# Sorting q by PSUM bank instead of by head halves, and turning the convolution weights later

## The chip, the cores and the metric

The kernel runs on one core of a Trainium2 chip. The engines named below are TensorE (PE, with its weight loads shown apart as PEld), VectorE (DVE), ScalarE (ACT), GpSimd (POOL) and SyncE (SP), which only issues transfers. Each engine takes its own instructions strictly in order. The metric is the device time of one execution in microseconds (us); lower is better.

## The reference, cut to what matters

Batch 8, 8 heads, sequence 576, head dimension 64, so that 8 x 64 = 512 columns go into the second part.

```python
kv  = einsum('bhsd,bhse->bhde', k, v)          # k^T v for each head, 64 x 64
out = einsum('bhsd,bhde->bhse', q, kv)         # "raw" in the kernel
rms = sqrt(mean(out * out, axis=-1) + 1e-6)
x   = out / rms * g_norm                       # then (B,H,S,D) -> (B,S,512)
gate = sigmoid(sum over k of conv_w[k] * x shifted by 4 - k)   # causal, 5 taps
val  = x @ w_val
result = (gate * val) @ w_out
```

The weights w_val, conv_w and w_out arrive as 64-bit floats and are made 32-bit on the chip ("narrowed") by a chain of integer and float steps on DVE and ACT. g_norm is folded into w_val and conv_w.

## The kernel before, in words

The program is one list of steps, the string `PLAN`. Each step is a small function (`sort_q 0 3` calls `sort_q(0, 3)`), and a step issues its instructions at once. So the list is the order in which each engine receives its work, written out by hand. A tile framework adds the waits between engines. All PSUM tiles come from one pool of 8 banks.

Work is done by batch; a batch has 5 chunks of the sequence, numbered 0 to 4. Chunks 0 to 3 have 128 tokens, chunk 4 has 64. Batch 0 (`WHOLE`) is treated differently from the others because it has nothing running ahead of it. Its steps at the head of the program, which the change and the prediction speak of, are these:

- `load_q_rows`, `load_half v`, `load_half k` load q, v and k of batch 0. v and k come in two halves (`v 0 0`, `v 0 1`); v is issued on ACT's queue, k on SP's. `stage_weight` loads a 64-bit weight: cw (conv_w with g_norm as its last row) on POOL's queue, w_val blocks on SP's. The loads of batch 1 follow on SP's queue.
- `turn_q_rows 0 j` (L478 to L489): PE transposes q for chunk j into one PSUM bank, `qTps` (L485). Of the bank's four blocks of 128 columns, the first two hold head half r = 0, the last two r = 1; the partitions 0 to 63 and 64 to 127 hold two different tokens of a pair (e = 0 and 1).
- `sort_q 0 j` (L494 to L506): four copies of 64 partitions from that bank into `qT` (L504), one for each r and e. Before the change ACT does the two copies with r = 0 and DVE the two with r = 1, for every chunk. For chunks 0 to 3 one copy has 256 elements a partition, for chunk 4 it has 128.
- `narrow_weight cw 0 n`: the narrowing of cw in eight parts. Parts 5, 6 and 0 are DVE's (L382, L387, L365), parts 1, 2 and 3 are ACT's (L370, L372, L374), parts 4 and 7 are DVE's (L377, L391), and the last one writes `cw`. The narrowing of w_val (`narrow_weight wval ...`) has the same lines with larger shapes.
- `start_warm`: matmuls on the identity that only keep PE occupied (L433).
- `kv_product 0 i` (L445): half i of k^T v, 72 matmuls into the two `kvps` banks. `kv_half 0 i` (L455): four copies on ACT that put this half into the block-diagonal `kvbd`.
- `raw_half 0 c i` (L533): q times k^T v for chunk c and half i of the heads. Only half 0 can run after `kv_half 0 0`; half 1 needs `kv_half 0 1`.
- `turn_cw` (L416): PE transposes `cw` into the bank `cwps`. `keep_cw` (L420 to L422): DVE takes g_norm (`gcol`) and the convolution weights (`cwT`) out of it.
- `square 0 c` (L552, ACT), `sums 0 c` (L565, DVE), `powers` (L573, POOL) and `normalise 0 c` (L582, DVE) make x; `turn_x` (L604, PE) and `keep_x` (L611, ACT) turn it for the second part.

In DVE's queue the three instructions of `keep_cw` come directly ahead of the narrowing of the first two w_val blocks (L382, L365, L387, L365, L382, L387), and these come ahead of `sums 0 3`. In ACT's queue `kv_half 0 1` is followed by parts 1 and 2 of the first w_val block (L370, L372) and then by `square 0 3`. PE goes from the raw matmuls of batch 0 straight to turning q of batch 1 (L491).

From about 30 us on the steady part follows: batch after batch of k^T v, raw, normalising, gate taps (L642, DVE), w_val products (L654, L703) and w_out products (L795, L741), interleaved by the list.

The lines that the change touches:

Of the kernel before, what the change touches and what calls it, by code (L numbers as in the profile page):

```python
# [20 lines left out]
load_half k 0 1; warm_up; stage_weight wval 1; stage_weight wval 0; start_warm 5 256; turn_q_rows 0 3;  # L21
turn_q_rows 0 2; turn_q_rows 0 0; turn_q_rows 0 1; turn_q_rows 0 4; sort_q 0 3; sort_q 0 2;
narrow_weight cw 0 5; narrow_weight cw 0 6; narrow_weight cw 0 0; sort_q 0 0; narrow_weight cw 0 1;
narrow_weight cw 0 2; narrow_weight cw 0 3; start_warm 3 256; kv_product 0 0; sort_q 0 4; kv_half 0 0;
sort_q 0 1; narrow_weight cw 0 4; narrow_weight cw 0 7; start_warm 1 256; raw_half 0 3 0; raw_half 0 4 0;
raw_half 0 2 0; turn_cw; keep_cw; kv_product 0 1; kv_half 0 1; raw_half 0 0 0; raw_half 0 1 0;
narrow_weight wval 1 5; narrow_weight wval 1 0; raw_half 0 3 1;
load_q_rows 1 1; narrow_weight wval 1 1; narrow_weight wval 1 6; narrow_weight wval 1 2; raw_half 0 4 1;
raw_half 0 2 1; load_q_rows 1 0; narrow_weight wval 0 0; narrow_weight wval 0 5; square 0 3; stage_weight wval 3;
# [180 lines left out]
def kernel(  # L210
# [11 lines left out]
    nc = tc.nc  # L222
# [45 lines left out]
    cw = const.tile([NK * K + 1, P], FP32, name="cw")  # L268
# [193 lines left out]
    def new_qT(b):  # L462
        if ("qT", b) not in st:
            st["qT", b] = work.tile([P, HP, S], FP32, tag="qT", name=f"qT{b}")
        return st["qT", b]
# [28 lines left out]
    def sort_q(b, j):  # L494

        m = min(HB, NB - j * HB)
        qT, pq = new_qT(b)[:].rearrange("p h (n t) -> p n h t", t=TB), st["pq", b, j][:].rearrange(
            "p n (h t) -> p n h t", t=TB)
        if b not in WHOLE:
            nc.scalar.copy(out=qT[:, j * HB:j * HB + m], in_=pq[:, 0:m])  # L500
            return
        for r in range(2):
            for e in range(2):
                (nc.vector.tensor_copy if r else nc.scalar.copy)(  # L504
                    out=qT[r * D:(r + 1) * D, j * HB + e:j * HB + m:2],
                    in_=pq[e * D:(e + 1) * D, r * 2:r * 2 + m // 2])  # L506

# [315 lines left out]
    def store(i, c, queue=nc.sync, blocks=range(HB)):  # L823
# [5 lines left out]
    steps = {f.__name__: f for f in (  # L829
        load_half, load_q, load_q_rows, stage_weight, narrow_weight, turn_cw, keep_cw, start_warm, warm_up,  # L830
        kv_product, kv_half, kv_copy, turn_q, turn_q_rows, sort_q, raw_half, raw_pair, raw_tail, square, sums, powers, normalise,
        turn_x, keep_x, turn_blocks, move_blocks, halo, gate_start, gate_tap, gate_end, val_product, keep_val, gated,
        val_sums, x_sums, val_fast, val_keep, out_product, keep_out, weight_sums, token_sums, fast_product, fast_keep,
# [36 lines left out]
```

## Time and profile before

| | us |
|---|---|
| median of 3 runs | 305.26 (305.22 to 305.46) |
| the profiled execution, its own time | 305.03 |
| its span, first to last instruction | 303.3 |
| PE busy | 292.9 (97% of the span) |
| PEld busy | 226.1 (75%) |
| DVE busy | 273.3 (90%) |
| ACT busy | 194.0 (64%) |
| POOL busy | 114.1 (38%) |

How to read the lines that follow: the profile gives one execution. A line of the instructions in order of time has the start in us from the span's first instruction, the length of the group, the engine, the line of the kernel (L504 is line 504), the operation, `out<-in` by the names of the tiles, the shapes (partitions x elements), how many instructions are merged, and in brackets how long the engine had been idle and what released it. PE's matmuls are pipelined, so their lengths overlap. Busy shares are means over the whole span; PE, DVE and ACT sit idle mostly in the first 30 us and at the very end.

### The profile page before, as it was taken

The page shows a single profiled execution, that of the slowest core. Times are in us where ns is not written, and L with a number is a line of the kernel's source. Part 1 is how long each engine was busy: PE and PEld are TensorE (multiplying, and loading weights), DVE is VectorE, ACT ScalarE, POOL GpSimd, SP SyncE. Part 2 cuts the span into 40 slices and gives each one's busy share as a digit, 9 for nine tenths or more (in the row PEclk, how much of TensorE's full clock was granted, in tenths as well). Part 3 has the DMA queues.
Part 4 walks back from the last instruction along what each step waited for, and adds up shares of the span by engine and source line. Part 5 has one row for each costly group of instructions (what it writes and reads, how often), then busy time and mean ns, then how long its engine had stood idle before and what let it go on. Part 6 is the DMA issues. An engine that isn't in the chain of part 4 may idle for free.

```text
span 303.3 us, 8782 instructions
## 1 busy us (share of the span) xinstructions
PE 292.9 (97%) x3333; PEld 226.1 (75%) x3333; DVE 273.3 (90%) x484; ACT 194.0 (64%) x604; POOL 114.1 (38%) x127
## 2 busy tenths in 40 slices
PE   8898999999999999999999999999999999999993
PEld 4596777787787875877778757787877588888582
DVE  1689999999999999999999999999999999999612
ACT  2679989999668654983586547682888354534220
POOL 3028073416659127265328452245536631000000
PEclk9999999999999999999999999999999999999999
DMA  7999996098469756989689477927411621112423
GB/s 274 396 400 322 278 283 166 20 281 242 130 166 352 215 143 157 285 223 267 175 238 279 126 214 189 341 57 219 108 43 35 173 73 36 35 46 61 104 69 104
DMA packets 32073, 55.51 MB, mean 183 GB/s; under 512 B 6166, under 2 KB 14358, under 8 KB 32032
## 3 DMA queue, kind: packets, MB, share of 16 engines
q1 hardware_dynamic: 29520, 49.76, 55.8%
q0 software_dynamic: 1632, 3.17, 3.9%
q10 hardware_dynamic: 880, 2.03, 1.9%
q8 instruction: 26, 0.43, 0.6%
q14 instruction: 15, 0.12, 0.2%
HBM read 39.21 MB, written 9.44 MB: 160 GB/s over the span
## 4 chain that ended last, share of the span: by engine, by line
PE 84%; DVE 6%; ACT 5%; DMA 2%; issue 2%; DVEq 0%; ACTq 0%; SPq 0%
PE a L795 18%; PE cb L795 14%; PE va L703 13%; PE val L654 11%; PE vc L703 6%; PE raw L521 5%; PE kvps L445 5%; PE out L741 5%; PE vb L703 4%; PE xTps L604 2%; DMA qs<-in_q_dram 2%; DVE gate L642 2%; DVE xs L688 1%; ACT sq L552 1%; PE raw L533 1%
## 5 line engine op out<-in xcount | busy, mean ns | idle before, releaser
L573 POOL TENSOR_TENSOR rt<-ss,mhalf 128x8 f32<-128x8 f32 (+3 forms) x38 | 68.5, 1810 | 101.2 <-DVE ss L565 101.0
L642 DVE SCALAR_TENSOR_TENSOR gate<-xT,cwT,gate 128x576 f32<-128x576 f32 x128 | 102.1, 811 | 1.0
L592 ACT ACTIVATE x<-raw,rt 128x64 f32<-128x64 f32 x252 | 55.8, 351 | 6.7 <-POOL rt L573 3.7
L625 POOL DMA_DIRECT2D xT<-y x48 | 26.4, 557 | 25.5 <-DVE ot L805 14.0
L654 PE MATMUL val<-xT,wval 128*128 128x288 f32 x128 | 33.4, 412 | 0.0
L795 PE MATMUL a<-wsum,sums 128*128 128x256 f32 x128 | 32.4, 382 | 0.0
L649 ACT ACTIVATE gate<-gate 128x576 f32<-128x576 f32 x32 | 22.0, 693 | 11.4 <-DVE gate L642 11.0
L654 PEld LDWEIGHTS val<-xT,wval 128*128 128x128 f32 x128 | 23.5, 190 | 6.9 <-DVE wval L391 0.5
L795 PEld LDWEIGHTS a<-wsum,sums 128*128 128x128 f32 x128 | 24.0, 190 | 4.1 <-issue 0.6
L556 ACT ACTIVATE sq<-raw 128x256 f32<-128x256 f32 (+1 forms) x70 | 22.2, 402 | 7.4 <-PE raw L521 7.1
L703 PE MATMUL va<-xs,vsum 128*128 128x288 f32 x96 | 26.6, 409 | 0.0
L636 ACT ACTIVATE gate<-xT,cwT 128x576 f32<-128x576 f32 x32 | 25.2, 811 | 1.4 <-DVE gv L667 1.3
L565 DVE TENSOR_REDUCE ss<-sq 128x8 f32<-128x520 f32 (+1 forms) x40 | 24.8, 630 | 1.4 <-ACT sq L552 1.0
L667 DVE TENSOR_TENSOR gv<-gv,gate 128x576 f32<-128x576 f32 x32 | 23.7, 752 | 0.9 <-ACT gate L649 0.6
L703 PEld LDWEIGHTS va<-xs,vsum 128*128 128x128 f32 x96 | 18.0, 190 | 5.2 <-ACT x L592 0.4
L632 POOL COPY xT<-xT 128x124 f32<-128x124 f32 x32 | 17.1, 575 | 9.8 <-ACT xT L611 9.8
L521 PEld LDWEIGHTS raw<-kv,qT 64*64 64x64 f32 x1008 | 16.4, 134 | 5.3 <-issue 3.0
L445 PEld LDWEIGHTS kvps<-v,k 64*64 64x64 f32 x1008 | 15.8, 135 | 4.0 <-issue 1.8
L521 PE MATMUL raw<-kv,qT 64*64 64x64 f32 x1008 | 18.7, 221 | 0.0
L445 PE MATMUL kvps<-v,k 64*64 64x64 f32 x1008 | 17.4, 220 | 0.0
L795 PE MATMUL cb<-wsum,sums 128*128 128x256 f32 x64 | 16.9, 386 | 0.1
L795 PE MATMUL cb<-wout,gv 128*128 128x256 f32 x64 | 16.8, 385 | 0.0
(114 smaller groups left out, 539.0 us busy)
## 6 DMA issues: line engine op xcount, KB each, us to landing
qs<-in_q_dram SPq DMA_DIRECT2D x96, 140.0 KB, 3.9
out_dram<-ot SPq DMA_DIRECT2D x140, 64.0 KB, 1.7
k<-in_k_dram SPq DMA_DIRECT2D x14, 576.0 KB, 6.2
v<-in_v_dram SPq DMA_DIRECT2D x12, 576.0 KB, 6.9
xT<-y SPq DMA_DIRECT2D x48, 64.0 KB, 2.5
xT<-y POOLq DMA_DIRECT2D x48, 64.0 KB, 2.9
y<-in_moe_w_val_dram SPq DMA_DIRECT2D x4, 512.0 KB, 11.2
w_wout<-in_moe_w_out_dram SPq DMA_DIRECT2D x4, 512.0 KB, 7.6
```

What stands on the lines that cost most here:

```text
L445: nc.tensor.matmul(st["kvps", b][s][r * D:(r + 1) * D, i], st["k", b, i][rows, r, cols], st["v", b, i][rows, r, cols], start=(j == 0), sto ...
L521: nc.tensor.matmul(st["raw", b, c][r][cols, to * D:(to + 1) * D], st["qT", b][rows, hp, first:first + D], kvs[b % 2][rows, hp, :], start=T ...
L565: nc.vector.reduce_sum(out=st["ss", b][:, FIRST[c]:FIRST[c] + n], in_=st["sq", b, c][:, 0:n], axis=AX.X)
L573: nc.gpsimd.tensor_tensor(out=st["rt", b][:, which], in0=st["ss", b][:, which], in1=mhalf[:, which], op=ALU.pow)
L592: nc.scalar.activation(out=x[:, to * D:(to + 1) * D], in_=raw[:, h * D:(h + 1) * D], func=AF.Copy, scale=root[:, to:to + 1])
L625: (nc.sync if i % 2 else nc.gpsimd).dma_start(out=xTs[b % 2][i * TB:(i + 1) * TB, :, first:first + P], in_=y[a * TB:(a + 1) * TB, i])
L636: nc.scalar.activation(out=gate[:], in_=xTs[b % 2][:, jt, HALO:SX], func=AF.Copy, scale=cwT[:, K - 1, jt:jt + 1])
L642: nc.vector.scalar_tensor_tensor(out=gate[:], in0=xTs[b % 2][:, jt, tap * TB:tap * TB + S], scalar=cwT[:, tap, jt:jt + 1], in1=gate[:], op ...
L654: nc.tensor.matmul(val[:], wval[:, kc, jt * P:(jt + 1) * P], xTs[b % 2][:, kc, HALO + n * SV:HALO + (n + 1) * SV], start=(kc == 0), stop=( ...
L667: nc.vector.tensor_tensor(out=both, in0=both, in1=st["gate", b, jt][:], op=ALU.mult)
L703: nc.tensor.matmul(st[bank, "val", b, mj][:], weights_[:, k], tokens()[:, k], start=(n in (0, 1, 3) and k == 0), stop=(k == NK // 2 - 1), ...
L795: nc.tensor.matmul(st[bank, i, p], tokens()[:, k], weights_[:, k], start=(n < 2 and k == 0), stop=(k == NK // 2 - 1), skip_group_check=True)
```

## The change

Two things change, both in batch 0 at the head of the program.

First, `sort_q` chooses the engine by chunk, so by PSUM bank: DVE makes all four copies of chunks 1 and 2, ACT all four of chunks 0, 3 and 4. The list moves `sort_q 0 1` ahead of `kv_half 0 0` and `sort_q 0 4` behind it.

Second, the order of raw and k^T v changes. Before: raw of chunks 3, 4, 2 (half 0), then `turn_cw`, `keep_cw`, the second k^T v, `kv_half 0 1`, raw of chunks 0 and 1. After: raw of chunks 3, 2, 0, then the second k^T v, `turn_cw`, `keep_cw`, `kv_half 0 1`, raw of chunks 1 and 4. The rest of the list is the same.

```diff
-narrow_weight cw 0 2; narrow_weight cw 0 3; start_warm 3 256; kv_product 0 0; sort_q 0 4; kv_half 0 0;
-sort_q 0 1; narrow_weight cw 0 4; narrow_weight cw 0 7; start_warm 1 256; raw_half 0 3 0; raw_half 0 4 0;
-raw_half 0 2 0; turn_cw; keep_cw; kv_product 0 1; kv_half 0 1; raw_half 0 0 0; raw_half 0 1 0;
+narrow_weight cw 0 2; narrow_weight cw 0 3; start_warm 3 256; kv_product 0 0; sort_q 0 1; kv_half 0 0;
+sort_q 0 4; narrow_weight cw 0 4; narrow_weight cw 0 7; start_warm 1 256; raw_half 0 3 0; raw_half 0 2 0;
+raw_half 0 0 0; kv_product 0 1; turn_cw; keep_cw; kv_half 0 1; raw_half 0 1 0; raw_half 0 4 0;
 narrow_weight wval 1 5; narrow_weight wval 1 0; raw_half 0 3 1;
...
         for r in range(2):
             for e in range(2):
-                (nc.vector.tensor_copy if r else nc.scalar.copy)(
+                (nc.vector.tensor_copy if j in (1, 2) else nc.scalar.copy)(
                     out=qT[r * D:(r + 1) * D, j * HB + e:j * HB + m:2],
                     in_=pq[e * D:(e + 1) * D, r * 2:r * 2 + m // 2])
```

## The prediction

> **What bounds the kernel now.** I read the page's busy shares first, then busy time by stretch, then the instructions in order of time on VectorE (DVE), ScalarE (ACT) and TensorE (PE) over the first 25 us, and last what SyncE's (SP's) queue waited for.
>
> The page, and the stretch from 32 to 80 us (busy time and count of PE, weight loads, DVE, ACT, POOL; clock; DMA share; GB/s):
> ```profile
> PE 292.9 (97%) x3333; PEld 226.1 (75%) x3333; DVE 273.3 (90%) x484; ACT 194.0 (64%) x604; POOL 114.1 (38%) x127
> ...
> 32.00:80.00 48.00, 47.98 (x664) 37.48 (x654) 47.75 (x83) 44.75 (x143) 19.47 (x14) 1.00 0.72 201
> ```
> From 32 us on PE and DVE are both full, in a written-out order that the change leaves alone there. What the head gains or loses reaches the end only as the same shift of both. The head is where both still idle. DVE in order of time (start, length, and in brackets the idle time before and what ended it):
> ```profile
> 7.64 1.75 DVE L504 COPY qT<-qTps 64x256 f32<-64x256 f32 x4 [5.92 <-ACT qT L504]
> ...
> 10.12 0.86 DVE L504 COPY qT<-qTps 64x256 f32<-64x256 f32 x2
> 11.96 0.59 DVE L504 COPY qT<-qTps 64x128 f32<-64x128 f32 x2 [0.99 <-ACT qT L504]
> 13.63 0.86 DVE L504 COPY qT<-qTps 64x256 f32<-64x256 f32 x2 [1.07 <-ACT qT L504]
> ...
> 14.82 0.28 DVE L391 SCALAR_TENSOR_TENSOR cw<-ot_cw,wexp_cw 20x128 f32<-20x128 f32 x1
> 15.44 0.16 DVE L420 TENSOR_SCALAR gcol<-cwps 128x1 f32<-128x1 f32 x1 [0.35 <-PE cwps L416]
> ...
> 19.69 0.70 DVE L565 TENSOR_REDUCE ss<-sq 128x8 f32<-128x520 f32 x1 [0.96 <-ACT sq L552]
> ```
> Each DVE copy of a bank begins 20 to 30 ns after ACT's last copy of the same bank: the two never read one bank together. The last idle time over 0.2 us is the 0.96 us before L565 (sums of chunk 3) at 19.69; after it DVE runs packed. So the start of that instruction dates everything after it. It waits for ACT's square:
> ```profile
> 6.86 2.29 ACT L504 COPY qT<-qTps 64x256 f32<-64x256 f32 x6 [3.13 <-PE qTps L485]
> 10.12 0.40 ACT L370 ACTIVATE wexp_cw<-wexp_cw,biases 20x128 uint32<-20x128 uint32 x1 [0.98 <-DVE wexp_cw L365]
> ...
> 11.40 0.53 ACT L504 COPY qT<-qTps 64x128 f32<-64x128 f32 x2
> 11.96 0.87 ACT L455 COPY kvbd<-kvps 64x64 f32<-64x64 f32 x4
> ...
> 16.66 0.87 ACT L455 COPY kvbd<-kvps 64x64 f32<-64x64 f32 x4 [3.07 <-PE kvps L445]
> 17.56 0.72 ACT L370 ACTIVATE wexp_wval<-wexp_wval,biases 128x512 uint32<-128x512 uint32 x1
> ```
> The square comes 1.50 us after the start of the L370 at 17.56, which stands behind the second kv_half (16.66), which waits for PE's second k^T v. PE:
> ```profile
> 12.43 2.16 PE L533 MATMUL raw<-kvbd,qT 128*128 128x128 f32 x12 [0.91 <-ACT kvbd L455]
> 15.20 0.21 PE L416 MATMUL cwps<-ident,cw 21*128 21x21 f32 x1 [0.61 <-PE raw L533]
> 15.34 1.28 PE L445 MATMUL kvps<-v,k 64*64 64x64 f32 x72
> 16.54 3.72 PE L533 MATMUL raw<-kvbd,qT 128*128 128x128 f32 x28
> ```
> The turning of cw (15.20) stands before the second k^T v and waits for cw, which DVE finishes at 15.10 because its sort of chunk 1 waited for ACT. So the second k^T v sits behind a sort that it doesn't need.
>
> **The change, part by part.** Sums go against the profiled execution: 305.03 us, of it 303.3 span; the median of the runs is 305.26, 0.23 above.
>
> *Copies by bank.* ACT loses 2+2 copies (r=0 halves of chunks 2 and 1) and gains 2+2 of chunks 3 and 0 and 2 of chunk 4: 8 x 0.367 + 4 x 0.26 = 3.98 against 3.46. DVE goes from 8 x 0.423 + 2 x 0.29 = 3.96 to 3.38. No copy of DVE stands behind ACT any more.
> - ACT takes chunks 3 and 0 in one run: 2.29 / 6 x 8 = 3.05, so 6.86 to 9.91.
> - DVE starts chunk 2 when PE has turned it, about 7.30 (the eighth of 18 transposes that take 2.40 from 5.95, each ending 0.27 after its start), and ends at 9.05. The three cw steps after it took 0.70 (9.39 to 10.09): 9.75. Chunk 1 follows at once and ends at 11.47.
> - ACT's three cw steps start at 9.94 (they waited for DVE until 10.12 before) and, at 1.27, end at 11.21. The first k^T v is done at 10.97, and chunk 4 is now behind kv_half: kv_half starts at 11.23 against 11.96, **0.73 earlier**. Cover: chunk 4's sort (4 x 0.27) moves to 12.10 to 13.20, where ACT sat idle (13.59 to 16.66); its reader, raw 4, now comes after the second k^T v.
> - DVE's last cw steps need ACT's (11.21) and run 11.50 to 12.10. cw is ready 3.0 us sooner.
>
> *Raw order.* Chunks 3, 2, 0 instead of 3, 4, 2. Raw starts at 12.43 - 0.73 = 11.70 (PE's warm-up ends at 11.52). Chunk 3's two waits on kvbd cost the same 0.87; the second and third chunks have 128 columns: about 0.63 each with the 0.2 us hand-over the trace shows between chunks. Second k^T v starts at 11.70 + 0.87 + 2 x 0.63 = 13.83 against 15.34, **1.51 earlier**.
>
> *cw turned behind k^T v.* In the trace the 72 matmuls take 1.20 to the next start, so cwps starts at 15.03 instead of 15.20, and L420 at 15.28 instead of 15.44: **only 0.16 earlier**. L420 to L422 stand on DVE ahead of wval's narrowing (L382, L365, L387 and so on), so DVE now idles from 12.10 to 15.28, and the narrowing is 0.16 earlier: L365 of the first weight ends at 16.57 instead of 16.73. ACT is through kv_half at 15.99, 1.54 earlier, but its L370 reads that L365: it starts at 16.60 instead of 17.56, **0.96 earlier**. Of 1.51 gained on PE, 0.55 is left at this wait.
>
> *The rest.* Square and sums follow at the old distances: L565 at 18.73. DVE's narrowings before it end at 18.57, so they don't hold it. The 28 raw matmuls run from 15.17 to 18.8; the next q loads needed there land by about 18.8 (the second issued 8.77, landed 10.0 later), and PE then waits anyway for normalise, which follows L565 through POOL's powers. PE, DVE and ACT then issue the same instructions as before, 0.96 earlier. Neither SP nor POOL issues anything differently; SP's loads of batch 2 wait for PE's turns of batch 1 and move along. Landings in the head are at full DMA share and do not move, but have room: the second half of batch 1's v lands after 11.3 us from 16.08, so about 27.4, for a product at 31.6 before, 30.7 after.
>
> Sum: 305.03 - 0.96 = 304.07; with 0.23 to the median, 304.3.
>
> *Unknown costs.* A copy with the other engine on another bank: DVE's second at 8.07 took 0.428 with ACT beside it, 0.418 to 0.428 elsewhere, so 0 to 0.05 in all; I take 0. Hand-over from raw to k^T v: between 0.11 (the pitch of matmuls) and 0.41 (the wait for data ahead of the first k^T v); I take the 0.2 seen between chunks. A head shift carried to the end: between 0 and all of it; I take all, being nearest to the row of 32 to 80 us with 0.25 us of DVE idle. A gain over 0.96 would need DVE's slack of 0.96 + 0.16 used fully: 1.12 at most. Together 303.9 to 304.7.
>
> *A landing.* The second k^T v is now asked for 1.5 us sooner. Its v half landed by 12.33, if the releaser is read rightly:
> ```profile
> SPq L312 <- DMA v<-in_v_dram: 2.0, 1, 2.0
> ```
> That is 1.5 us ahead of 13.83. The weight load issued on SP after both k halves at 2.18 landed 11.2 later, at 13.38, also ahead. What the trace proves outright is only that all was there at 15.34. The Trainium skill (DMA: Bandwidth & Descriptors, Queues, rings and completion order) says that completion is not first-in-first-out per issuing engine, so the later landing need not date the k half; but also that a DMA engine's semaphore write lands after all its earlier writes, across queues. By the first half the product could start as late as 15.33 and the time would be the 305.8 of the last rival below; by the second, which the 12.33 fits, 304.3.
>
> **The rivals.**
> - *The gain is given back.* DVE and PE run packed, but a later transfer or PSUM bank that doesn't move takes the 0.96 us: 305.2. For it: DMA is at full share up to 26 us. Against: from 26 to 60 us I find landings 3 us and more ahead of use (batch 2's last q quarter at 51.7 is turned at 60.4), and the later waits for stores are relative to DVE and ACT.
> - *More than forecast.* The 0.55 us that ACT waits shrinks, because the cw turn and L420 come sooner than I put them: up to the 1.12 of DVE's slack, 304.1; with raw's hand-overs at 0.11, too. Inside the forecast's range.
> - *Slower: DVE parks behind keep_cw.* DVE's queue now stands at L420 until the second k^T v is over. From L420's start it is 1.29 us to the end of the first L365 and, with 0.03 between, 2.13 from L370's start to L565's: 3.45 in all. So L565 is later than 19.69 as soon as L420 starts after 16.24, that is, if the second k^T v starts after 14.8. Only late data does that. At the latest start that the trace allows, 15.33, L420 is at 16.78 and the sums 0.54 late: 305.8.
> - *The change does not free DVE.* If the wait came from writing one tile qT rather than from reading one bank, DVE would still follow ACT. The changed kernel's instruction order speaks against it: its DVE copies wait for PE alone. 305.3 to 305.5.
>
> **How the numbers follow.** Forecast (with "more") 0.78; given back 0.10; parks 0.09; does not free 0.03. The forecast's own range is 303.9 to 304.7. About 0.2% (0.6 us) is what a measurement of this kernel can tell from no change. Faster by more than that: 0.76 (the forecast but for its upper edge). Within: given back, that edge and most of "not freed": 0.15. Slower: 0.09. The range reaches to the given-back case: 303.7 to 305.2.
>
> **What would show it.** In the changed profile: ACT's first group of copies is 8 long and ends near 9.9; DVE's first copy starts near 7.3 and waits for PE; kv_half near 11.2; the second k^T v near 13.8; L420 near 15.3 with some 3 us of idle before it, put down to cwps; ACT's L370 on wval near 16.6, now waiting for DVE; L565 near 18.7 with next to no idle before it; and PE's val, a and cb groups all about 1 us earlier to the end. It is wrong if the second k^T v waits for data, if L565 stays at 19.7, or if L565 is early and the same groups at 80 us or 200 us are not.

## The result, and the profile after

The changed kernel takes 304.4 us (median of 20 executions, 303.7 to 305.54), the kernel before 305.49 in the same comparison (20 executions, 305.2 to 306.56). The ratio is 0.9961, with a 95% interval of 0.9952 to 0.9971: faster by 0.4%, about 1.2 us (0.9 to 1.5 by the interval; the medians differ by 1.09). The forecast was 304.3, and 0.96 us of gain.

The profile that came with the result happens to be of the slowest of those 20 executions (305.54; its span is 303.8 us). So a second profile of the same kernel was taken (304.08 us, span 302.3), and one of the kernel before beside it (305.45, span 303.6). These two are read here, as "changed" and "before"; what the first one showed in addition comes further down.

The instructions of the changed kernel in order of time, ACT first, then DVE, then PE:

```profile
6.78 3.02 ACT L504 COPY qT<-qTps 64x256 f32<-64x256 f32 x8 [3.05 <-PE qTps L485]
9.82 0.40 ACT L370 ACTIVATE wexp_cw<-wexp_cw,biases 20x128 uint32<-20x128 uint32 x1
...
11.11 0.88 ACT L455 COPY kvbd<-kvps 64x64 f32<-64x64 f32 x4
12.01 1.08 ACT L504 COPY qT<-qTps 64x128 f32<-64x128 f32 x4
14.68 0.88 ACT L455 COPY kvbd<-kvps 64x64 f32<-64x64 f32 x4 [1.59 <-PE kvps L445]
16.15 0.72 ACT L370 ACTIVATE wexp_wval<-wexp_wval,biases 128x512 uint32<-128x512 uint32 x1 [0.60 <-DVE wexp_wval L365]
```
```profile
7.21 1.73 DVE L504 COPY qT<-qTps 64x256 f32<-64x256 f32 x4 [5.50 <-PE qTps L485]
...
9.67 1.73 DVE L504 COPY qT<-qTps 64x256 f32<-64x256 f32 x4
...
14.83 0.16 DVE L420 TENSOR_SCALAR gcol<-cwps 128x1 f32<-128x1 f32 x1 [2.81 <-PE cwps L416]
...
18.29 0.69 DVE L565 TENSOR_REDUCE ss<-sq 128x8 f32<-128x520 f32 x1 [0.17 <-ACT sq L552]
```
```profile
11.59 1.83 PE L533 MATMUL raw<-kvbd,qT 128*128 128x128 f32 x12
13.35 1.28 PE L445 MATMUL kvps<-v,k 64*64 64x64 f32 x72
14.56 0.23 PE L416 MATMUL cwps<-ident,cw 21*128 21x21 f32 x1
```

And of the kernel before, in its second profile, the points that answer to them on ACT, PE and DVE:

```profile
11.85 0.87 ACT L455 COPY kvbd<-kvps 64x64 f32<-64x64 f32 x4
...
17.46 0.72 ACT L370 ACTIVATE wexp_wval<-wexp_wval,biases 128x512 uint32<-128x512 uint32 x1
```
```profile
12.33 2.16 PE L533 MATMUL raw<-kvbd,qT 128*128 128x128 f32 x12 [0.91 <-ACT kvbd L455]
15.09 0.21 PE L416 MATMUL cwps<-ident,cw 21*128 21x21 f32 x1 [0.61 <-PE raw L533]
15.23 1.28 PE L445 MATMUL kvps<-v,k 64*64 64x64 f32 x72
```
```profile
15.34 0.16 DVE L420 TENSOR_SCALAR gcol<-cwps 128x1 f32<-128x1 f32 x1 [0.35 <-PE cwps L416]
...
19.59 0.69 DVE L565 TENSOR_REDUCE ss<-sq 128x8 f32<-128x520 f32 x1 [0.96 <-ACT sq L552]
```

What to see: DVE's copies no longer wait for ACT but for PE (the brackets), the two engines sort side by side, and kv_half starts at 11.11. The kernel before had it at 11.85. The second k^T v comes 1.88 us earlier, L420 only 0.51 earlier with 2.81 us of idle DVE ahead of it, L370 waits 0.60 us for DVE and comes 1.31 earlier, and L565 is 1.30 us earlier. In this pair of profiles that is the whole gain: the last instruction of DVE stands at

```profile
298.45 0.42 DVE L818 COPY ot<-a 128x256 f32<-128x256 f32 x1 [0.17 <-PE a L795]
```
in the kernel before, and in the changed one at
```profile
297.10 0.42 DVE L818 COPY ot<-a 128x256 f32<-128x256 f32 x1 [0.17 <-PE a L795]
```
which is 1.35 earlier. Taken every 20 us on DVE, the shift between the two profiles lies between 1.30 and 1.39 us throughout.

### The profile page after: what moved, and what is told of

It is laid out like the page before. It is cut to its first block, busy times and chain, and to the rows that moved or that the text cites. A ratio compares the mean times of both kernels' runs of the same rounds, so it can differ in the third digit from the quotient of the medians.

```text
span 303.8 us, 8778 instructions
## 1 busy us (share of the span) xinstructions
PE 293.9 (97%) x3333; PEld 226.6 (75%) x3333; DVE 273.0 (90%) x482; ACT 194.4 (64%) x606; POOL 114.5 (38%) x127
## 4 chain that ended last, share of the span: by engine, by line
PE 76%; DMA 8%; SPq 5%; ACT 4%; DVE 3%; issue 2%; DVEq 0%
PE a L795 15%; PE va L703 13%; PE cb L795 12%; PE val L654 11%; PE vc L703 6%; PE kvps L445 4%; PE raw L521 4%; DMA out_dram<-ot 4%; PE out L741 4%; PE vb L703 3%; DMA qs<-in_q_dram 3%; SPq L625 2%; PE xTps L604 2%; DMA v<-in_v_dram 2%; SPq L322 1%
## 5 line engine op out<-in xcount | busy, mean ns | idle before, releaser
L565 DVE TENSOR_REDUCE ss<-sq 128x8 f32<-128x520 f32 (+1 forms) x40 | 24.7, 627 | 0.8 <-ACT sq L556 0.7
L470 DVE STREAM_TRANSPOSE qT<-qs 128x512 f32<-128x512 f32 x24 | 16.6, 693 | 0.5 <-DMA qs<-in_q_dram 0.5
L805 DVE TENSOR_TENSOR ot<-cb,ot 128x512 f32<-128x512 f32 x16 | 10.9, 681 | 6.8 <-DMA out_dram<-ot 4.1
```

What stands on the lines that cost most here:

```text
L565: nc.vector.reduce_sum(out=st["ss", b][:, FIRST[c]:FIRST[c] + n], in_=st["sq", b, c][:, 0:n], axis=AX.X)
```

## The experiments

Absolute times in the head move by some tenths between executions: the 18 q transposes at its start take 2.18 us in one and 2.70 in another. So L565 is given here as its distance from the end of the q transposes (start plus length of PE's L485 group); it is 11.33 us for the kernel before (second profile; 11.34 in the first) and 10.03 for the changed one (9.95 in the first). The last column is the ratio of times to the kernel before on the same chip. A difference in L565 comes from one profile each, a difference in time from several executions.

| kernel | L565 after q | against before | median us (before) | ratio, 95% interval |
|---|---|---|---|---|
| before | 11.33 | | | |
| changed, second run | 10.03 | -1.30 | 304.24 (305.69) | 0.9956, 0.9942 to 0.9970 |
| banks alone | 11.02 | -0.31 | 305.05 (305.18) | 0.9994, 0.9985 to 1.0003 |
| order alone | 10.99 | -0.34 | 305.33 (305.18) | 1.0006, 0.9995 to 1.0017 |
| cw turn still later | 11.24 | -0.09 | 305.29 (305.69) | 0.9988, 0.9975 to 1.0002 |
| cw turn back ahead | 9.61 | -1.72 | 303.75 (305.18) | 0.9955, 0.9943 to 0.9967 |
| keep_cw later on DVE | 9.84 | -1.49 | 303.51 (305.18) | 0.9944, 0.9932 to 0.9956 |
| exponents early | 9.06 | -2.27 | 303.46 (305.69) | 0.9931, 0.9911 to 0.9951 |

The theory under test: one chain (first kv_half, raw, second k^T v, cw turn, L420, L365, L370, square, L565) dates everything after it, and a shift of L565 goes to the end one to one (that part is taken up again further down, where the profiles are compared at 200 us). The rivals: one of the two parts alone carries the gain, or more than about 1 us of shift is not carried.

**Banks alone.** The sort by banks, with the old list of steps:

```diff
-                (nc.vector.tensor_copy if r else nc.scalar.copy)(
+                (nc.vector.tensor_copy if j in (1, 2) else nc.scalar.copy)(
```


> One part alone: the sort is shared by banks, but the list of steps is that of the kernel before (sort of chunk 4 ahead of the first kv_half, the cw turn ahead of the second k^T v, raw in the order 3, 4, 2). Theory (a chain of kv_half, raw, second k^T v, L365, L370, L565 dates the rest): ACT now makes all four copies of chunk 4 ahead of kv_half, which starts near 12.6 instead of 11.96; raw starts near 13.0, but cw is ready at 12.5, so the cw turn (15.1) and the second k^T v (15.2) stand where they were. L565 at 19.5 against 19.69: a gain of 0.1 to 0.2 us, 305.1 to 305.2 where before has 305.3. Rival (the freed copies are the gain, the order of steps is not needed): most of the 1.0 us is there, 304.4.

The time is the same within what can be told. ACT has all four copies of chunk 4 (1.07) ahead of kv_half, and kv_half, and so the first raw, starts 3.92 us after the q transposes, 0.33 later than in the kernel before (11.85 less 8.26). In this kernel's profile:

```profile
11.00 1.07 ACT L504 COPY qT<-qTps 64x128 f32<-64x128 f32 x4
12.08 0.87 ACT L455 COPY kvbd<-kvps 64x64 f32<-64x64 f32 x4
```
Freeing DVE alone takes the copies' waits away but not their place ahead of kv_half. The 0.31 us that L565 still gains comes from the cw turn, which no longer waits for cw (0.61 before); that outweighs the 0.33.

**Order alone.** The new list of steps, with the old sort:

```diff
-                (nc.vector.tensor_copy if j in (1, 2) else nc.scalar.copy)(
+                (nc.vector.tensor_copy if r else nc.scalar.copy)(
```


> The other part alone: the changed list of steps with the old sort by head halves. Theory: DVE's halves of chunks 1 and 4 wait for ACT again, cw is ready near 14.8, and kv_half starts 0.2 later than before, because chunk 1's copies (0.75) stand ahead of it where chunk 4's (0.53) stood. The second k^T v starts near 14.8 (15.34 before), the cw turn near 16.0, L420 near 16.2, and L565 at 19.65 against 19.69: no change, 305.2 to 305.3. Rival (moving the cw turn is the gain): L565 near 18.7 and 304.3.

No gain in time either. DVE follows ACT again, and a wait goes up where DVE is behind:

```profile
11.93 0.86 DVE L504 COPY qT<-qTps 64x256 f32<-64x256 f32 x2 [1.20 <-ACT qT L504]
13.38 0.59 DVE L504 COPY qT<-qTps 64x128 f32<-64x128 f32 x2 [0.59 <-ACT qT L504]
```
L565 is 0.34 earlier in the profile where the theory had 0.04, because the first raw group is 0.37 shorter than the theory put it (see "Raw order" below). The median shows nothing of the 0.34 (0.15 us faster to 0.5 slower). In the profile, DVE keeps the lead until past 200 us and loses it near 219, where it waits for ACT, which had waited for a store to land:

```profile
217.41 0.37 ACT L807 COPY ot<-a 128x256 f32<-128x256 f32 x1 [0.81 <-DMA out_dram<-ot]
```
```profile
219.38 0.82 DVE L642 SCALAR_TENSOR_TENSOR gate<-xT,cwT,gate 128x576 f32<-128x576 f32 x1 [0.83 <-ACT gate L636]
```
In the second profile of the changed kernel that copy of ACT doesn't wait:

```profile
215.67 0.39 ACT L807 COPY ot<-a 128x256 f32<-128x256 f32 x1
```

The two parts alone make no measurable difference in time and 0.31 and 0.34 us in L565, together they make 1.2 us and 1.30: the banks bring the copies side by side, and the new order is what then moves chunk 4's copies out from ahead of kv_half.

**The cw turn still later.** Behind raw of chunks 1 and 4:

```diff
-raw_half 0 0 0; kv_product 0 1; turn_cw; keep_cw; kv_half 0 1; raw_half 0 1 0; raw_half 0 4 0;
+raw_half 0 0 0; kv_product 0 1; kv_half 0 1; raw_half 0 1 0; raw_half 0 4 0; turn_cw; keep_cw;
```


> The changed kernel with the cw turn and keep_cw put still later, behind raw of chunks 1 and 4: one cause made worse. Theory (DVE's queue stands at L420, and L565 follows L420 by 3.45 us): the turn comes 1.0 us later, L420 1.0 later, L565 1.0 later, and the gain is gone: 305.2 to 305.5 where before has 305.2. Rival (ACT's earlier second kv_half is what counts, and DVE has room): at most 0.2 us lost, 304.3.

DVE's idle ahead of L420 grows from 2.81 to 4.03 us, ACT's ahead of L370 from 0.60 to 1.82, though kv_half ends as early as in the changed kernel:

```profile
16.10 0.16 DVE L420 TENSOR_SCALAR gcol<-cwps 128x1 f32<-128x1 f32 x1 [4.03 <-PE cwps L416]
```
```profile
14.72 0.87 ACT L455 COPY kvbd<-kvps 64x64 f32<-64x64 f32 x4 [1.60 <-PE kvps L445]
17.42 0.72 ACT L370 ACTIVATE wexp_wval<-wexp_wval,biases 128x512 uint32<-128x512 uint32 x1 [1.82 <-DVE wexp_wval L365]
```
Most of the gain is gone (304.24 to 305.29, where the kernel before has 305.69); what is left, 0.4 us, can't be told from nothing by its interval. So an earlier second kv_half alone is worth little or nothing; L420's place on DVE decides.

**The cw turn back ahead of the second k^T v:**

```diff
-raw_half 0 0 0; kv_product 0 1; turn_cw; keep_cw; kv_half 0 1; raw_half 0 1 0; raw_half 0 4 0;
+raw_half 0 0 0; turn_cw; keep_cw; kv_product 0 1; kv_half 0 1; raw_half 0 1 0; raw_half 0 4 0;
```


> The changed kernel with the cw turn and keep_cw put back ahead of the second k^T v; all else as changed. Theory: in the changed kernel cw is ready at 12.5, so the turn need not wait there any more: it costs PE 0.15 us, L420 comes at 14.0 instead of 15.25, and DVE narrows the first weight 1.2 us sooner (L365 ends near 15.4). ACT's L370 is then bound by the second kv_half (ends near 16.1), not by DVE: 16.15 instead of 16.57, L565 at 18.3 instead of 18.70. 0.4 us faster than the changed kernel, 303.9 to 304.1 where that has 304.4. Rival (turning cw behind k^T v is what brings the gain): 305.2.

L565 is 0.42 earlier after q than in the changed kernel, as expected. L370 now follows kv_half directly:

```profile
14.77 0.88 ACT L455 COPY kvbd<-kvps 64x64 f32<-64x64 f32 x4 [1.76 <-PE kvps L445]
15.67 0.73 ACT L370 ACTIVATE wexp_wval<-wexp_wval,biases 128x512 uint32<-128x512 uint32 x1
```
303.75 against 305.18 is 1.4 us of gain. The comparisons' intervals (0.9943 to 0.9967 here, 0.9942 to 0.9970 for the changed kernel on another chip) don't separate the two kernels; that turning cw behind k^T v is not what brings the gain they do show.

**keep_cw later on DVE**, the turn unmoved:

```diff
-raw_half 0 0 0; kv_product 0 1; turn_cw; keep_cw; kv_half 0 1; raw_half 0 1 0; raw_half 0 4 0;
+raw_half 0 0 0; kv_product 0 1; turn_cw; kv_half 0 1; raw_half 0 1 0; raw_half 0 4 0;
...
-narrow_weight wval 0 6; narrow_weight wval 1 3; sums 0 3; load_half k 1 0; square 0 2; square 0 4;
+narrow_weight wval 0 6; narrow_weight wval 1 3; keep_cw; sums 0 3; load_half k 1 0; square 0 2; square 0 4;
```


> The changed kernel with keep_cw alone moved in DVE's queue, from ahead of the first weight's narrowing to just ahead of the sums of chunk 3; the turn stays behind the second k^T v. Theory (the 0.6 us that ACT idles in the changed kernel ahead of L370 is DVE parked at L420): DVE narrows from the landing of the weight (about 13.4), L370 follows kv_half at 16.0 instead of 16.57, L565 at 18.1 instead of 18.70: 0.55 us faster than the changed kernel, 303.8 where that has 304.4. Rival (a shift of the head by more than 1 us is not carried, because landings or SP's queue hold the middle): L565 is as early, the time stays at 304.4.

L370 came at 15.49, right behind kv_half, so the 0.6 us was indeed DVE standing at L420. But L565 gained only 0.19 more, because DVE waited for the second weight, which landed at 15.94, with L420 and L565 behind:

```profile
15.96 0.43 DVE L365 TENSOR_SCALAR wexp_wval<-y 128x512 uint32<-128x512 uint32 x1 [1.18 <-DMA y<-in_moe_w_val_dram]
...
17.48 0.16 DVE L420 TENSOR_SCALAR gcol<-cwps 128x1 f32<-128x1 f32 x1
...
18.02 0.68 DVE L565 TENSOR_REDUCE ss<-sq 128x8 f32<-128x520 f32 x1
```
One parking place had been traded for another. The landing was no exception: in six of the ten profiles that block lands at 15.9 to 16.0, in four at 14.6 to 14.9. The time, 303.51 (1.7 us under the kernel before, 1.3 to 2.1 by the interval), says that a shift above 1 us is carried.

**Exponents early.** The turn back ahead, two narrowing steps ahead of keep_cw, and ACT's first exponent step ahead of the second kv_half:

```diff
-raw_half 0 0 0; kv_product 0 1; turn_cw; keep_cw; kv_half 0 1; raw_half 0 1 0; raw_half 0 4 0;
-narrow_weight wval 1 5; narrow_weight wval 1 0; raw_half 0 3 1;
-load_q_rows 1 1; narrow_weight wval 1 1; narrow_weight wval 1 6; narrow_weight wval 1 2; raw_half 0 4 1;
+raw_half 0 0 0; turn_cw;
+narrow_weight wval 1 5; narrow_weight wval 1 0; keep_cw; kv_product 0 1; narrow_weight wval 1 1; kv_half 0 1; raw_half 0 1 0; raw_half 0 4 0;
+raw_half 0 3 1;
+load_q_rows 1 1; narrow_weight wval 1 6; narrow_weight wval 1 2; raw_half 0 4 1;
```


> The cw turn ahead of the second k^T v, the first two narrowing steps of the first weight ahead of keep_cw on DVE, and ACT's first exponent step (L370) ahead of the second kv_half: ACT works where it idles in the changed kernel (13.5 to 15.1). Theory: L565 another 0.4 to 0.6 us ahead of the kernel with only the cw turn moved back. But there PE already reached the transposes of x (L604) without waiting, because the q loads of batch 1 land near 18.7 and turning them takes 2.8; so that the head can give no more: 0 to 0.3 us under that one's 303.75, 1.4 to 1.7 under the kernel before. If L565 alone dated the end (no new bound): 2.0 us under the kernel before, 303.2.

In this kernel's profile (its line numbers are one higher from this place on):

```profile
14.23 0.72 ACT L371 ACTIVATE wexp_wval<-wexp_wval,biases 128x512 uint32<-128x512 uint32 x1 [1.23 <-DVE wexp_wval L366]
14.98 0.87 ACT L456 COPY kvbd<-kvps 64x64 f32<-64x64 f32 x4
```
```profile
17.25 0.69 DVE L566 TENSOR_REDUCE ss<-sq 128x8 f32<-128x520 f32 x1 [0.41 <-ACT sq L553]
```
ACT does exponent work where it had idled. 303.46 against 305.69 is 2.2 us faster (1.5 to 2.7 by the interval), with a lead of L565 of 2.27: by the medians about all of it is carried. Not so in the profiled execution (303.82): there DVE stands 2.34 us ahead of the kernel before's second profile at 20 us and 1.55 at the end. The caution that PE's transposes of x would be a new bound was wrong as to the time. PE does reach them without waiting at 21.60, but the next wait in its order goes too: the second run of q transposes starts unhindered (in the changed kernel it waited 0.47 us for ACT). This version beats both kernels: five of its six executions are shorter than the shortest of the changed kernel's twelve on the same chip (303.84).

**The changed kernel once more, and the kernel before once more.**

> The changed kernel once more, for a second profile of it. In its first profile L565 came 0.99 us earlier and everything stayed 0.99 earlier to 78 us; then 0.33 was lost at a w_out product near 79 us, 0.22 near 89, 0.61 near 115 where DVE waited for q of a later batch, and 0.26 near 254, so that the execution itself ended late (305.54, where the median is 304.4). Theory (those losses are of that one execution, where a store held SP's queue for 8 us): here the shift of the head stays through the middle, and the execution ends about 1 us ahead of the kernel before's. Rival (the earlier head runs into landings that don't move, and half of it is usually lost): the same losses at the same places again. Time about 1.0 us under the kernel before on the same chip.

> The kernel before once more, for a second profile to hold the others against, because the landing of the first q loads differs by some tenths between executions. Sums of chunk 3 (L565) near 19.7 and 11.3 us after the q transposes end; no change of time.

In this pair the theory held: a shift of 1.3 to 1.4 us from 20 us to the end, as shown above. The first profile differs from this one most at 115 us. There DVE waited for q of a later batch; the chain of waits of that profile leads to it through SP's queue:

```profile
93.50 8.28 DMA out_dram<-ot
...
110.31 4.46 DMA qs<-in_q_dram
...
114.80 0.05 DVEq L470
```
This store took 8.28 us to land; in the other nine profiles the same one took 6.60 to 6.88. SP waited 1.4 us for it. SP's next stores were issued behind it at 101.86 (99.33 in the second profile, which at that place is some 1.0 us ahead), the q loads after them at 105.53 (103.97), and DVE waited 0.52 us for the data; 0.61 us of the shift was lost there. The other losses of that execution (0.33 near 79 us, 0.22 near 89, 0.26 near 254) were not traced to a cause.

So the head's gain can be lost again in the middle, and that was not one odd execution. Held against the second profile of the kernel before, instruction by instruction, DVE is ahead by (us; a minus is behind):

| profile | near 20 us | near 200 us | last instruction |
|---|---|---|---|
| changed, first | 0.89 | -0.26 | -0.23 |
| changed, second | 1.30 | 1.31 | 1.35 |
| banks alone | 0.42 | 0.45 | 0.38 |
| order alone | 0.49 | 0.50 | -0.13 |
| cw turn still later | 0.04 | 0.03 | 0.27 |
| cw turn back ahead | 1.78 | 1.66 | 1.70 |
| keep_cw later on DVE | 1.59 | 1.71 | 2.01 |
| exponents early | 2.34 | 1.95 | 1.55 |

Three of the eight lose 0.6 to 1.1 us on the way. "Exponents early" loses some near 79 and 89 us, where the first profile of the changed kernel lost too, and 0.6 near 219, where "order alone" did: there DVE's wait for ACT is 0.87 and ACT's for a store 0.84. The kernel before loses as well: its own second profile falls 0.3 behind its first near 233 us. So one profile doesn't tell what a head shift is worth; the times of several executions do, and all of them but "order alone" hold the lead of L565 within their intervals.

## Why the prediction was right

The direction, the place and the mechanism were right. The size was too small: 0.96 us in L565 where the two second profiles show 1.30; the time gained was 1.2 us in the first comparison and 1.35 (0.44%) in the second. The intervals of these times (0.9 to 1.5 and 0.9 to 1.8) hold 0.96 as well; it is the profiles that show it too small. That 304.3 came within 0.1 of the measured 304.4 is in part luck: the forecast started from 305.26, the comparison's kernel before took 305.49, and the smaller gain made up for most of that. The first profiles, too, agree with 0.96 by luck alone: there L565 stands at 18.70 against 19.69, 0.99 earlier, but the q transposes had ended 0.40 later in the changed kernel's execution (8.75 against 8.35); counted from them the lead is 1.39.

- *Copies by bank.* Right. ACT's run of 8 took 3.02 (forecast 3.05), DVE's chunks 1.73 each (1.75), no copy waited for ACT, kv_half came 0.74 earlier (0.73). The rival that DVE is not freed fell with the brackets: ACT and DVE now write the one tile qT side by side. One reading was loose: a copy of DVE began 32 or 33 ns after ACT's last of the bank on chunks 3, 4 and 1 only; on chunks 2 and 0 DVE was busy until later. Whether the chip or only the waits put into the program kept the two engines apart in one bank, no run shows.
- *Raw order.* This is the step that was mis-sized. I gave each later chunk 0.63 us, "with the 0.2 us hand-over the trace shows between chunks", and put the second k^T v 2.13 us after the first raw. It came after 1.76. The hand-overs of 0.2 belong to chunk 4 alone, whose product is 64 wide instead of 128. Start to start, PE's raw matmuls in the kernel before take 0.21 into chunk 4, 0.16, 0.10 and 0.11 inside it, and 0.21 and 0.21 out of it, and 0.11 or 0.12 all through chunks 2 and 0 in the changed kernel. "Banks alone" (with chunk 4 in the middle) needs 2.09 from the first raw to the next kind of matmul, "order alone" (without) 1.76. The cost has not gone: the second group of 28 raw matmuls now has chunk 4 twice and takes 4.05 instead of 3.72, which I had not counted, but there PE has 0.35 us of slack ahead of the transposes of x. The profile lists chunk 4's matmuls as 128*64 and the others as 128*128. The Trainium skill says why it may be (TensorEngine Tiling (Array Packing), Key Properties): changing the tiling mode drains the engine. These rows agree, and price a change there and back at some 0.3 us; that it is the drain, no run shows apart. I had the lower end (0.11) among the unknown costs, as "more than forecast", without seeing what the 0.2 was. My upper bound of 1.12 us was wrong with it: it took L420 as only 0.16 earlier.
- *cw turned behind k^T v.* Right in kind: L420 sits far ahead of its data, and L370 waits for DVE (0.60; forecast 0.61). With the 0.37 us of the step above taken off, L420 came 0.51 earlier instead of 0.16, and L370 and L565 1.31 and 1.30 instead of 0.96.
- *The rest.* Right in the second pair of profiles: L565 dates everything, one to one, to the last instruction. Not so in each execution: "given back" happened in full in the first profile, where DVE at 200 us is 0.18 later than in the kernel before's first profile. By the sign that I had set myself (the same groups at 200 us), that execution alone would have spoken against the forecast. The reading under it was wrong: the 0.96 us ahead of L565 is not DVE's last idle time over 0.2 us, for the same profile has 0.52 at 211.19, 0.41 at 216.12 and 0.60 at 233.31.
- *A landing.* Nothing waited for the second half of k and v: no wait of PE at 13.35, and the k half had landed at 12.21 in the second profile of the changed kernel. The rules on completion of the Trainium skill (DMA: Bandwidth & Descriptors, Queues, rings and completion order) thus made no difference here.
- *DVE parks behind keep_cw.* The rival named the right place. It did not make the kernel slower, but "the cw turn still later" shows how near it is: with L420 1.21 us later after q than in the changed kernel, all but 0.09 us of the lead of L565 is gone. And the changed kernel pays for it: with the 0.6 us that ACT waits there removed, L565 came 0.42 sooner ("cw turn back ahead") and 0.19 ("keep_cw later"). So the third part of the change, turning cw later, cost some of what the other two brought.

## What to carry to other kernels

Where two engines share the reading of several PSUM banks, as ACT and DVE did here, give each engine whole banks; but then look again at what stands ahead of the next link of the chain on each engine, because here neither the split nor the order was worth anything measurable alone. An instruction that waits for a late result parks everything behind it in its engine's queue, as L420 did on DVE here (2.81 us), so put work whose data is there already ahead of it ("exponents early", which does that and also uses ACT's idle time, was worth another 0.8 us). And time saved in a head where engines idle can be worth its full length when all engines run packed afterwards: here the medians gave about that, while single executions lost 0.6 to 1.1 us of it again.

## What the runs showed of the hardware beyond that

- A 64-wide matmul group between 128-wide ones costs PE some 0.3 us in all (1.83 against 2.16 us for 12 matmuls), although it has half the columns of weights.
- The landing of one and the same load in the head moves by more than a microsecond between executions: the second w_val block landed at 14.7 us in the first profile of the kernel before and at 16.0 in its second (14.6 to 14.9 in four of the ten profiles, 15.9 to 16.0 in six, nothing between). A plan that reads it just in time gains less than its one profile promises.
- Stores of 64 KB land after 1.7 us in the median, but the one issued at 91 to 94 us took 6.60 to 6.88 in nine profiles and 8.28 in the tenth; there what was queued behind it on SP reached DVE late 21 us after its issue.
